# Turning the local attention result with whole-array matmuls, under a new hand-written order of steps

## The chip, the cores and the metric

The kernel runs on one core of a Trainium2 chip. The metric is the device time of that core in microseconds (us), the median of three runs. The profile is one execution taken by the hardware profiler. Its engines are PE (TensorE matmuls; PEld are its weight loads), DVE (VectorE), ACT (ScalarE), POOL (GpSimd) and SP (the queue that issues nearly all DMAs).

## The reference, cut to what matters

```python
# 8 batches, 8 heads, 576 positions, head size 64, factor 4
q_d, k_d, v_d = means over groups of 4 positions            # 144 positions
out_up   = repeat(softmax(q_d k_d^T / 8) v_d, 4)            # coarse attention
out_local = softmax(q k^T / 8 where |i - j| < 4) v          # band attention
x = out_up + out_local                                      # as (8, 576, 512)
theta = x @ w_theta
y = w_tok_r @ (x * cos(theta)) + w_tok_i @ (x * sin(theta)) # over positions
u = x + y
out = u + relu(u @ w_ch)
```

## The kernel before, in words

All eight batches run through the same chain of steps, and several batches are under way at once. What sets the order is a table written out by hand, `ORDER`: some 1190 words, each one step. The first two letters are the kind of step, the rest says where it goes: for steps on PE the PSUM bank or the two banks that it writes, for copies and casts the engine (v DVE, a ACT, g POOL), for loads the staging slot. The k-th word of a kind is the k-th batch and piece of that kind. `pin()` ties each engine's instructions to that order, so every engine, SP too, works strictly in the order of the words. A step whose input is late holds up all that stands behind it on its engine.

The steps of a batch, in the words used below:

- Loads on SP into 16 staging slots: `lk`, `lq` (k and q, 288 KB, L287), `lv` and `lw` (the two halves of a piece of v, 128 KB each, L347). A slot is loaded anew once its earlier content is cast.
- Casts to bf16: `ck`, `cq` (L295), `cv` (L396). `tp` turns k or q on PE (nine 128x128 transposes, L302), `ev` copies it out of PSUM (L315). `kd`, `qd` are the sums of four positions (two POOL instructions, L329 and L332 or L335, or one on DVE, L321).
- Coarse attention: `pv`, `vd` (means of v: PE L404 and L407, copy L412 and L415), `sd`, `ed` (scores L426, exponential on ACT L437), `nd`, `xn` (L447, L452; division on DVE), `xd`, `xc`.
- Local attention: `ps`, `ex` (scores L482, exponential L490), `mk` (band mask, on DVE L505 or on POOL L503 and L505), `po` (times v, L515), `nm` (division on DVE, L523 and L524, into `tmp`).
- `xt` (L537) turns the local result so that channels are on partitions, into PSUM. `xa` (L545, DVE) adds the coarse result on the way to `xT`.
- The rest: `th`, `cs` (theta on PE L556, cosine and sine on ACT), `xm`, `zz` (product with x), `mx`, `ua` (mixing over positions, 64 groups of nine 128x288 matmuls, L636, and the sum on DVE L641), `up`, `du`, `ch`, `rl` (the last matmul L666 and its relu on DVE L674), `st` (stores), `ht`, `rt` (the same for the last 64 positions of two batches).
- `wm` are matmuls of zeros that fill PE while it has nothing to do (L764).

Matmuls of `ps`, `sd`, `po` and `xt` use 64x64 quarters of the array, four at a time; nearly all others use the whole array.

Of the kernel before, what the change touches and what calls it, by code (L numbers as in the profile page):

```python
# [57 lines left out]
kcg l10 l11 l12 l13 kcv lk4 lq5 c1a wm7e0 kcg c1g t101 lk6 lk7 ckg c1a ckg c1v t123 e1a kcv e1v wm737 tp01 x12 cqa x13
lq8 x14 cka x15 cqg evv cva lk9 tp67 ckg cvv cva lqa lqb tp01 lk1 cqg x14 cva wm521 evv evv cqa qdv tp23 cva la3 eva
pv47 vda wm624 ps01 kdg la6 ps23 ex kdv ckg lq4 ex wm656 wm717 lq2 ps01 qdg lk5 sd67 mkv ckv cqg sd45 po23 ed lk8 cag  # L60
ed ex po67 lq9 lba nm cba nd45 nm nd23 xn cag mkg cqa tp01 po67 xn po45 nm lkb eva xd0 mkg ckg lq7 cka xca la1 po23 nm
tp67 cag xt45 la0 xt01 nm lb3 lb4 lb5 cqg lbc xa lba lb2 xt23 xa eva tp67 lb8 cqg lb1 caa ts th4 kdg cs cbg xm5 xa lv7
evv lw th0 th2 lv0 cbv lw zz cbg tt3 xm4 lv3 cs cbg cbv ct cbg cbg cs lvb lw lw wp0 wcv wp1 wcv ztg wp5 th3 wp1 lv8
wcv xm2 cbg xm0 zz zp7 tp45 cs qdg wp3 wp6 zz wcv lw zz wcv wcv zca eva wp7 wcv wp1 wca te wp0 wcv ps34 ps56 ex ex
ps12 mx0 lq1 cvg lk2 lka mx7 lqc mx3 qdv cvg ua lk7 ex ua lk0 mkv mkv kdg sd67 po45 nm sd12 lq4 cva lk5 lk9 cvg cvg ed
ed mx0 ua ua lq3 pv67 po45 po23 nm mx0 vda mkg nd67 lk8 nd45 lkb nm xn xn lq6 ckg ckg tp12 mx3 po45 ua lca ua nm cqg
cqg tp67 eva eva xd0 ckg ckg up1 lq7 po23 lvc xcv nm tp45 xt67 cqg mx0 cqg xt23 eva xt45 lv4 qdg kdg uca lw lv0 lw lw
lv3 lv1 lw lw xa xa tp67 cka ts ckg ckg th1 th2 xa th5 lk8 xm4 evv cs cqg xm1 ckv th3 zz tt4 up6 lq6 lqb cs zz tp12
xm7 ua cs ucv ct cs cqg eva te ztv xm6 zz zz mx0 ua tp34 zp7 tp56 ps12 zcv mx7 mx0 ex cvv kdg evv eva lk7 lk9 cvg lk4
qdg ua up7 uca sd12 mkv ps34 po56 ex ua ccv lcc lc5 kdg nm mkv mx0 sd34 ed po56 cvg cvg ua cqg mx7 nm ua ed mx0 ua lk2  # L70
cka cqg ps67 lqd lq0 cva po45 nm lca ex po23 ckg ckg nm pv01 lvb mx6 vda lk6 utv lw tp45 eva lv1 lw cca ccv nd01 nd23
ua xn xn qdg tp67 mx5 eva lv8 lv9 cqg cqg lw lw ccg ps34 qdg ps67 ua ps12 kdv ex ex xd0 lva xca lw mkg mkg lqc lq0 ch5
rl ckg ckg cvg cvg ch3 sd67 xt45 mkg ed rl ex ts mx0 xa xt67 po45 lv5 th1 cs xa nm ua tp23 th7 up4 up1 ucv xt56 xa mkv
lv4 ch0 eva po56 po23 cvg lq2 tt4 uca th1 cs th7 nm st nm xm2 lqb rl lq1 zz lqd ct cvg xm6 lw cqg ch5 cs zz cs cqa te
up0 up1 rl sd23 ucv po67 ch4 nm rl ch0 rl ucv tp67 lv7 ed cvg pv45 vdv lk8 lk9 eva st st tp23 eva xm0 ztg lk0 lka lw
xm1 zz zz zp7 ch6 zca lvc lv3 kdg nd45 xn nd23 ckg tp01 cva xn qdg utg mx7 cka ps23 rl kdg eva ps01 ua po45 mx6 up7 ex
ex lw lw lv8 nm qdg lw cqg po45 cqg ucv lvb lv2 lw sd23 sd01 lv5 ed mx7 lw lw ua tp23 nm xd4 ed ckg ckg xca st evv
tp01 eva mx6 mkg xt45 xt23 ua ua cva cvg cvg xt01 cka ts cvg xa xa mx7 th6 xa po45 nm pv23 tt0 th1 lk4 xm4 st st mkg
th5 vdv st cs nd23 ua zz ct cqg cqg ztg tp67 th4 cs dt po01 cs cs te xn evv po23 mx5 kdg qdg xm4 xm6 mx7 nm ps01 ex nm
ps23 ua lvd ua ex ch5 ps01 ex qdg zz lw lw xm7 zz rl kdg zp6 zz mkg nd23 xn lv1 lva lv3 mx5 zca sd67 lw ps01 ex po34  # L80
mx2 ua lw ed tp01 sd67 cva nm po34 eva cvv cvg ed lw up5 uca ua mx2 cvg nm cvg lvc xd3 ua pv04 xcv lk7 lk0 mx7 lq9 lq6
lq2 lqd lq8 lqb lq5 ckg ckg vda lq7 lw xt56 mkv cqg cqg po34 lk4 xt01 xa xa ch2 st cva ts lv6 th5 up6 ckg xm0 nm th1
# [5 lines left out]
evv mx1 ztg xd2 up0 ua cs ch3 rl cs te mx4 ch7 qdg ps56 rl xcv ua mx1 ex cvg po23 po45 ua uca ps67 ex ht1 nm nm st st
rt cva ss mx0 ua po67 xt45 nm ps23 st xa ex ts du kdg th1 xm0 xm7 cs th6 cs xm4 zz zz zz ch5 rl kdg mx7 ua th0 po67 nm
cs te xt45 xa sd12 ch3 xm0 ch7 ch4 xt56 st ed sd12 mkg mkg ed ts zz dz lw mx0 lv1 du du cvv lw cvg th1 cs rl uta mx3  # L90
st rl rl xa dxb ua po45 po67 pv02 nm nm ua du mx1 vda ch4 dx mkg ua po23 po01 po67 rl sr nm mx5 ua mx4 tt5 dx1 du nm
nm nd23 xn nd01 st mx6 th7 mx2 cs xn xd3 mx0 ua ua xcv ua ua xt67 utv ct dx st st xt45 xt23 xa ch1 rl th0 ch6 ch1 ch7
cs xa xa tt0 zz zz th2 th3 cs st du du ch4 rl zz zz ztg ct dz rl mx2 mx0 mx1 cs ua ua st dxe dx ht0 ua th1 cs th3 dx7
dx zz st st mx2 rl mx1 ua ua cs zz dt mx3 mx1 mx2 zz zz ztg dz mx7 ua mx3 du du du mx6 rt ua ua utg ua st rl du st mx7
mx4 ua ua ua sr mx7 mx6 mx5 ua ua ua du du ua ch7 ch6 ss ch5 rl rl ch7 ch6 ch4 ch3 du du st uta dt sta rl st rl ht7
ch2 sta rl st rl sta rl st rt ssa sr rl sta rm su k0
"""


# [1 line left out]
def kernel(  # L101
# [161 lines left out]
    at = {}  # L263
# [261 lines left out]
                                in0=ps[:, :, :, 0:D], in1=r.unsqueeze(3).to_broadcast([P, 2, 4, D]), op=ALU.mult)  # L525

    def xt(b, u, w):
        ps = at["xt", b, u] = pair(w).rearrange("p k (x n) -> p (k x) n", x=2)
        for i, c in enumerate(UNITS[u]):
            t = tmp[(NCH * b + c) % NTMP]  # L530
            for g in range(2):
                n = 2 * c + g
                lo = STEP * n - W0[n]
                for j in range(4):
                    for hf in range(2):
                        r = slice(W * hf, W * hf + W)
                        nc.tensor.matmul(out=ps[W * (j % 2):W * (j % 2) + W, 2 * hf + j // 2,  # L537
                                                CH * i + STEP * g:CH * i + STEP * g + OWN[n]],
                                         lhsT=t[r, g, D * j:D * j + D], rhs=ident[r, W * hf + lo:W * hf + lo + OWN[n]],
                                         start=True, stop=True)  # L540

    def xa(b, u, w):
        lo = 2 * CH * u
        cnt = min(2 * CH, S - lo)
        nc.vector.tensor_tensor(  # L545
            out=xT[b % 2][:, :, lo:lo + cnt].rearrange("p e (m j) -> p e m j", j=4),
            in0=at.pop(("xt", b, u))[:, :, 0:cnt].rearrange("p e (m j) -> p e m j", j=4),
            in1=xdT[b % 2][:, :, lo // 4:(lo + cnt) // 4].unsqueeze(3).to_broadcast([P, 4, cnt // 4, 4]),
            op=ALU.add)


# [256 lines left out]
```

## Time and profile before

| | |
|---|---|
| time, median of 3 runs | 230.54 us (230.37 to 230.74) |
| span of the profiled execution | 232.2 us (a time of its own for it is not shown) |
| PE busy | 217.7 us, 94% |
| DVE busy | 187.7 us, 81% |
| ACT busy | 156.2 us, 67% |
| POOL busy | 145.0 us, 62% |
| DMA queue q1 | 81.9% of 16 engines' span |

PE is busy for nearly the whole span, so what counts is how much work PE has and where it waits. In the first 30 us it waits for loads and for the first batch's chain; behind that its waits are short and scattered. Busy time includes the time in which the last matmul of a group drains, so a step of PE is better read from the chain of waits, which runs from end to end. Differences in span are taken over to the median one to one.

### The profile page before, as it was taken

Reading aid. Unit: us, or ns where it says so; the run is one execution under the profiler, and the core shown is the slowest. Engines: PE = TensorE matmul, PEld = TensorE weight load, DVE = VectorE, ACT = ScalarE, POOL = GpSimd, SP = SyncE. Lnnn points to the kernel's source line nnn. Section 1 sums busy time; section 2 is a strip of 40 time slices with the busy share of each in tenths; the row PEclk is TensorE's granted clock in tenths of the full one; section 3 lists DMA queues with packets and bytes.
Section 4 is the critical chain, followed back from the end, with each engine's and each line's share of the span. In section 5 each row is a group of like instructions: output and inputs, shape, how many; then the busy total and the mean of one; then the engine's idle time right before and its main releaser. Section 6 shows DMA issues by size and latency. Waiting matters only on the chain.

```text
span 232.2 us, 9404 instructions
## 1 busy us (share of the span) xinstructions
PE 217.7 (94%) x3943; PEld 152.6 (66%) x3970; DVE 187.7 (81%) x367; ACT 156.2 (67%) x243; POOL 145.0 (62%) x192
## 2 busy tenths in 40 slices
...
GB/s 217 395 390 390 291 114 238 361 300 118 265 391 179 165 245 285 243 142 214 205 165 347 307 213 115 206 153 92 67 149 109 71 127 193 138 159 137 142 227 245
DMA packets 76795, 49.41 MB, mean 213 GB/s; under 512 B 61136, under 2 KB 61392, under 8 KB 76752
## 3 DMA queue, kind: packets, MB, share of 16 engines
q1 hardware_dynamic: 76096, 47.76, 81.9%
q10 hardware_dynamic: 656, 1.05, 1.3%
q8 instruction: 31, 0.51, 0.9%
...
## 4 chain that ended last, share of the span: by engine, by line
PE 60%; DMA 10%; POOL 10%; issue 6%; ACT 5%; DVE 4%; SPq 4%; DVEq 0%; POOLq 0%; ACTq 0%
PE PS L636 21%; PE PS L666 9%; PE PS L556 8%; DMA st<-in_q_dram 6%; PE PS L302 4%; POOL two L329 3%; PE PS L515 2%; SPq L347 2%; DMA st<-in_k_dram 2%; PE PS L537 2%; DMA ur<-uT 2%; POOL q_tm L295 2%; PE PS L482 2%; PE PS L447 1%; PE PS L595 1%
## 5 line engine op out<-in xcount | busy, mean ns | idle before, releaser
L636 PE MATMUL PS<-WT,z 128*128 128x288 bf16 x576 | 78.0, 287 | 0.0
L636 PEld LDWEIGHTS <-z 128*128 128x128 bf16 x576 | 53.9, 98 | 15.9 <-issue 1.3
L641 DVE TENSOR_TENSOR uT<-PS,xT 128x288 bf16<-128x288 f32 x64 | 28.6, 452 | 12.7 <-PE PS L636 10.9
L561 ACT ACTIVATE cs<-PS,pihc 128x512 bf16<-128x512 f32 x32 | 22.0, 689 | 21.1 <-PE PS L556 13.4
L556 PE MATMUL PS<-wth,xT 128*128 128x512 bf16 x116 | 30.8, 383 | 0.7 <-issue 0.2
L666 PE MATMUL PS<-wch,uT 128*128 128x512 bf16 (+1 forms) x122 | 29.8, 373 | 0.9 <-issue 0.6
L524 DVE TENSOR_TENSOR tmp<-PS,rl 128x512 bf16<-128x512 f32 x40 | 27.7, 692 | 1.4
L545 DVE TENSOR_TENSOR xT<-PS,xdT 128x928 bf16<-128x928 f32 (+1 forms) x24 | 22.3, 952 | 3.7 <-PE PS L537 2.3
L674 DVE SCALAR_TENSOR_TENSOR osb<-PS,ur 128x512 f32<-128x512 f32 x28 | 19.1, 687 | 7.1 <-DMA ur<-uT 3.0
L490 ACT ACTIVATE pm<-PS 128x1024 bf16<-128x1024 f32 (+1 forms) x24 | 20.5, 880 | 6.2 <-PE PS L482 6.1
L577 POOL TENSOR_TENSOR zT<-xT,cst 128x512 bf16<-128x512 bf16 x7 | 9.7, 1383 | 20.6 <-ACT cst L574 20.6
L295 POOL CAST k_tm<-st 128x576 bf16<-128x576 f32 x23 | 15.1, 668 | 11.2 <-DMA st<-in_k_dram 11.1
L396 POOL CAST v_w<-st 128x512 bf16<-128x512 f32 x21 | 13.3, 651 | 10.6 <-DMA st<-in_v_dram 10.5
L770 ACT ACT_TABLE_LOAD x15 | 19.2, 1283 | 0.3
L666 PEld LDWEIGHTS <-uT 128*128 128x128 bf16 x132 | 11.9, 98 | 11.2
L562 ACT ACTIVATE cs<-PS 128x512 bf16<-128x512 f32 x32 | 19.1, 597 | 0.0
L556 PEld LDWEIGHTS <-xT 128*128 128x128 bf16 x128 | 11.7, 99 | 10.6 <-issue 0.6
L295 POOL CAST q_tm<-st 128x576 bf16<-128x576 f32 x23 | 15.4, 686 | 4.9 <-DMA st<-in_q_dram 4.7
L503 POOL TENSOR_TENSOR pm<-pm,band 128x512 bf16<-128x512 bf16 x16 | 18.3, 1164 | 0.0
L329 POOL TENSOR_TENSOR two<-qT 128x576 f32<-128x576 bf16 x14 | 16.5, 1177 | 0.7 <-ACT qT L315 0.4
L620 DVE TENSOR_TENSOR z<-PS,cs 128x1024 bf16<-128x1024 bf16 x24 | 15.8, 684 | 0.5 <-ACT cs L562 0.3
L437 ACT ACTIVATE pd<-PS 128x864 bf16<-128x864 f32 x16 | 13.8, 889 | 2.5 <-PE PS L426 2.5
...
## 6 DMA issues: line engine op xcount, KB each, us to landing
...
st<-in_v_dram SPq DMA_DIRECT2D x70, 128.0 KB, 5.2
...
```

Source lines behind the costliest of these rows:

```text
L295: COPY[w](out=to, in_=of)
L329: nc.gpsimd.tensor_tensor(out=t, in0=src[:, :, 0:2], in1=src[:, :, 2:4], op=ALU.add)
L490: nc.scalar.activation(out=pm[(3 * b + u) % NPM][:, :, 0:n].rearrange("p e c j w -> p e (c j w)"), in_=at.pop(("ps", b, u))[:, :, 0:4 * W ...
L524: nc.vector.tensor_tensor(out=tmp[(NCH * b + c) % NTMP].rearrange("p g (j d) -> p g j d", d=D), in0=ps[:, :, :, 0:D], in1=r.unsqueeze(3).t ...
L545: nc.vector.tensor_tensor(out=xT[b % 2][:, :, lo:lo + cnt].rearrange("p e (m j) -> p e m j", j=4), in0=at.pop(("xt", b, u))[:, :, 0:cnt].r ...
L556: nc.tensor.matmul(out=ps, lhsT=xT[b % 2][:, dc, P * c:P * c + P], rhs=wth[:, dc, :], start=(dc == 0), stop=(dc == 3))
L561: nc.scalar.activation(out=t[:, 0, :], in_=ps, func=AF.Sin, bias=pihc, scale=1.0)
L562: nc.scalar.activation(out=t[:, 1, :], in_=ps, func=AF.Sin, bias=0.0, scale=1.0)
L636: nc.tensor.matmul(out=ps, lhsT=z[b % 2][:, j, P * dc:P * dc + P], rhs=WT[:, j, cols], start=(j == 0), stop=(j == 8))
L641: nc.vector.tensor_tensor(out=uT[b % 2][:, dc, cols], in0=at.pop(("mx", b, i)), in1=xT[b % 2][:, dc, cols], op=ALU.add)
L666: nc.tensor.matmul(out=ps[:, cols], lhsT=uT[b % 2][:, dc, P * c:P * c + P], rhs=wch[:, dc, cols], start=(dc == 0), stop=(dc == 3))
L770: nc.scalar.activation(out=idle, in_=pihc, func=TABLE[kind])
```

## The change

`xt` no longer uses quarters of the array. A chunk's results of eight heads lie on all 128 partitions: two groups of heads on the two halves. Before, each head and each of two position groups had a matmul of its own, 16 for a chunk. Now one matmul takes all 128 partitions and two heads' 128 channels, against two shifted copies of the identity side by side (2 x 58 columns): 4 for a chunk, each writing into one bank. The two halves that were in two banks lie in one bank now, so `xa` reads PSUM in another order. `ORDER` is a new table: new order, staging slots, PSUM banks and engines for copies and casts.

```diff
-mx7 ua cvg cvv uca te po01 nm qdg kdg qdg sd56 ed po23 ua ch4 rl xd0 ch1 ztg lw nm up7 ch4 uca xca po23 dz xt67 rl evg
+dk8 ct lqd cs zz cvg ucv ua tp34 eva mkg qdg kdg ckg cqv kdv th5 xm7 qdg mx6 zz xcv ua uca cs rl mx1 po67 ua po45 sd23
...
     def xt(b, u, w):
-        ps = at["xt", b, u] = pair(w).rearrange("p k (x n) -> p (k x) n", x=2)
+        ps = at["xt", b, u] = pair(w).rearrange("p k (x n) -> p k x n", x=2)
         for i, c in enumerate(UNITS[u]):
             t = tmp[(NCH * b + c) % NTMP]
             for g in range(2):
                 n = 2 * c + g
                 lo = STEP * n - W0[n]
-                for j in range(4):
-                    for hf in range(2):
-                        r = slice(W * hf, W * hf + W)
-                        nc.tensor.matmul(out=ps[W * (j % 2):W * (j % 2) + W, 2 * hf + j // 2,
-                                                CH * i + STEP * g:CH * i + STEP * g + OWN[n]],
-                                         lhsT=t[r, g, D * j:D * j + D], rhs=ident[r, W * hf + lo:W * hf + lo + OWN[n]],
-                                         start=True, stop=True)
+                for k in range(2):
+                    nc.tensor.matmul(out=ps[:, k, :, CH * i + STEP * g:CH * i + STEP * g + OWN[n]],
+                                     lhsT=t[:, g, P * k:P * k + P], rhs=identw[:, :, lo:lo + OWN[n]],
+                                     start=True, stop=True)
 
     def xa(b, u, w):
...
-            out=xT[b % 2][:, :, lo:lo + cnt].rearrange("p e (m j) -> p e m j", j=4),
-            in0=at.pop(("xt", b, u))[:, :, 0:cnt].rearrange("p e (m j) -> p e m j", j=4),
-            in1=xdT[b % 2][:, :, lo // 4:(lo + cnt) // 4].unsqueeze(3).to_broadcast([P, 4, cnt // 4, 4]),
+            out=xT[b % 2][:, :, lo:lo + cnt].rearrange("p (x k) (m j) -> p x k m j", k=2, j=4),
+            in0=at.pop(("xt", b, u))[:, :, :, 0:cnt].rearrange("p k x (m j) -> p x k m j", j=4),
+            in1=xdT[b % 2][:, :, lo // 4:(lo + cnt) // 4].rearrange("p (x k) m -> p x k m", k=2).unsqueeze(4)
+            .to_broadcast([P, 2, 2, cnt // 4, 4]),
             op=ALU.add)
```

The words for each engine count as follows: casts of v on POOL 21 before and 28 now, on ACT 13 and 8, on DVE 6 and 4; masks on POOL 14 and 13; filler matmuls of 512 columns 27 and 19, beside a few shorter ones. All else keeps its number of instructions, and most of it its engine.

Three places in the new order.

First place, the head: ACT's queue around the first batch's exponentials, before and then now (qT0 and kT0 are copies of the turned q and k, vd0 the means of v, pm0 and pm1 the exponentials of the local scores).

```order
L315 COPY qT0_64<-PS_61 128x1152
L412 CAST vd0_72<-PS_61 128x8x64
L415 CAST vd0_72<-PS_61 32x4x64 x2
L490 ACTIVATE pm0_83<-PS_61 128x1024
L490 ACTIVATE pm1_84<-PS_61 128x1024
```

In the new order, at the same place on ACT:

```order
L315 COPY kT0_62<-PS_61 128x2x576
L315 COPY qT0_64<-PS_61 128x1152
L261 CAST uT0_111<-st_126 128x576
L490 ACTIVATE pm0_83<-PS_61 128x1024
L490 ACTIVATE pm1_84<-PS_61 128x1024
```

The copies of vd0 went to DVE, and a cast of a token weight took their place.

Second place, POOL's queue ahead of the coarse scores of batch 6 (q_tm1 is the cast of its last q, k_tm2 that of a k of batch 7, qd0 and kd0 its sums), before:

```order
L295 CAST k_tm2_76<-st_126 128x9x64
L295 CAST q_tm1_78<-st_126 128x9x64
L396 CAST v_w0_70<-st_126 128x8x64
L329 TENSOR_TENSOR two_80<-qT0_64 128x576
L335 TENSOR_TENSOR qd0_68<-two_80 128x288
L329 TENSOR_TENSOR two_80<-kT0_62 128x580
L332 TENSOR_TENSOR kd0_66<-two_80 128x2x5x29
```

In the new order, on POOL:

```order
L396 CAST v_w0_70<-st_126 128x8x64
L505 TENSOR_TENSOR pm1_84<-pm1_84,band_131 128x2x256
L329 TENSOR_TENSOR two_80<-qT0_64 128x576
L335 TENSOR_TENSOR qd0_68<-two_80 128x288
L329 TENSOR_TENSOR two_80<-kT0_62 128x580
L332 TENSOR_TENSOR kd0_66<-two_80 128x2x5x29
L295 CAST k_tm0_74<-st_126 128x9x64
```

The cast of batch 6's last q is now on ACT, away from the k of batch 7. The sums' last word, `qdg`, stood directly ahead of the scores `sd56` (the line of `ORDER` above); now two groups of `mx` and two `po` stand between it and `sd23`.

Third place, POOL's queue ahead of the means of v of batch 3 (pm2 is the mask of its second local unit, v_w1 the casts of its v, of which `pv` needs all five), before:

```order
L503 TENSOR_TENSOR pm2_85<-pm2_85,band_131 128x512 x2
L396 CAST v_w1_71<-st_126 128x8x64 x2
L295 CAST q_tm0_77<-st_126 128x9x64
L396 CAST v_w1_71<-st_126 128x8x64
L577 TENSOR_TENSOR zT_110<-xT0_101,cst_109 128x512
```

In the new order, on POOL:

```order
L503 TENSOR_TENSOR pm2_85<-pm2_85,band_131 128x512 x2
L396 CAST v_w1_71<-st_126 128x8x64 x2
L295 CAST k_tm0_74<-st_126 128x9x64
L295 CAST k_tm1_75<-st_126 128x9x64
L329 TENSOR_TENSOR two_80<-kT0_62 128x580
L332 TENSOR_TENSOR kd0_66<-two_80 128x2x5x29
L396 CAST v_w1_71<-st_126 128x8x64
```

Behind these, one k cast, the mask pm3, one v cast, two q casts and the fifth v cast follow on POOL before `pv` of batch 3 can start; before, the fifth v cast came three casts after the mask pm2.

More of the change, by code (lines that the diff above doesn't have):

```diff
@@ L57 @@
 ORDER = """
[L58 to L82, printed above, removed]
@@ L88 @@
[L88 to L96, printed above, removed]
+l10 l11 l12 l13 lk4 c1a lk5 ckg lk6 lq7 lq0 lk8 c1a c1a lq1 wm053 t101 e1v c1a ckg wm231 t123 cqg e1v cqg kcg wm431
@@ new lines @@
+tp01 x14 x15 lq2 x12 x13 cka evv cvv kdv cvv kcv x16 ckg cva cqg cva tp01 cqg lk9 la3 lb4 lb5 lb6 lk7 lq0 wm710 tp23
+kcg cva eva wm717 tp01 pv45 eva eva wm711 ps23 kcv kdv cba lb8 lq1 qdg la2 lba qdg lbb lq4 vdv ex mkv cbv ps01 wm751
+sd45 cbv po23 ex lkc ed ckg ckg lad po01 cbg cqg cqg la9 lb7 lk8 cbg cag lq0 nm mkv sd67 nm lb1 lba ps45 tp23 ed ex
+nd67 lv3 xn nd45 tp01 po67 xn cag mkg cbg cag nm eva ts eva wp2 po34 xd5 xca nm wcv cqa kdg qdg cbg wp6 lvb lvd lw lw
+xt01 cqg xa xt45 wca xa caa po23 wp7 lk0 wp6 th0 cbg th1 nm cbg cka wca xt23 xm7 th4 wcv ckv cs xa cs zz tp56 tt2 th7
@@ new lines @@
+xm3 cs ct tp01 xm2 wp4 cs evv lw ztg lva lv1 eva zz xm3 wp5 wp7 lw zz lw wp2 zp6 wca ps01 zz wcv te wp5 ex zcv wcv wcv
+ps34 wcv cvv kdg mx7 qdg mx2 ps01 mkv ckg cvg ex po56 ex cvg cvg cvg ua ua nm mx3 sd01 lk0 lqb ed po45 sd67 mx2 mkv
+po01 ed nm po45 ua pv36 mx7 nm nm ua ckg xt01 vda lkd lq3 nd34 cqa ts nd56 ua xn xn mx7 tp23 lk7 lq8 ua xd5 lqa lk1
+lvc xcv lk9 lw xa lqb lk0 lq4 lk2 mx7 lc6 lq5 lve eva cka cka lv7 mkg lw cqg xt45 cqg tp23 lw lv8 po01 th6 xa tp45 eva
+lqd lw lv3 th2 xm3 ua nm lw lkf cs xt67 qdg ckg evv cqa th0 cs cs tp45 lc1 xm2 eva lka xa zz xm3 tt6 th7 mx0 ps45 xm1
@@ new lines @@
+cvg kdg cqg ckv zz zz cqv ct cs ztv ckg ckg kdg up6 lv2 lq0 lcb lc4 lk9 qdg zp7 tp23 zz cvg zcv ucv ua ex eva mx1 ua
+tp67 eva te mkv tp45 evv mx1 sd23 ps67 po45 mx0 nm up4 ex cvv ed cva ua mx5 uca ua mkv sd12 po67 ps34 cqg kdg nm kdg
+ccg ckg cqg ua ckg ed ex cva utg mx0 po67 po45 nm ua pv23 nm vda mx1 up0 ua ucv tp67 nd45 tp01 eva xn nd23 mx6 ps45 xn
+ps23 lw lv8 lqf lkd lka lk3 cca qdg ccg cqg qdg eva lw lvb cca mkv ua xd0 up1 ex lw lq4 xcv ch7 lv0 lv1 lw lq6 uca rl
+xt45 xa xt01 mx6 ch7 cqg ckg ex xa sd45 ps01 ua ex po23 ed utv mkv th6 nm cs th0 xt12 rl tp34 xa mkg cvg cvg ch7 evv
```

26 lines of the change are left out of this document (22 added, 4 removed).

## Prediction

> **What bounds the kernel now.** I read the page first, then the busy time by stretches, the chain of waits, and the timeline where PE waits.
>
> ```profile
> PE 217.7 (94%) x3943; PEld 152.6 (66%) x3970; DVE 187.7 (81%) x367; ACT 156.2 (67%) x243; POOL 145.0 (62%) x192
> 20.00:25.00 5.00, 3.64 (x102) 3.15 (x101) 4.54 (x13) 3.83 (x6) 5.00 (x7) 0.99 1.05 337
> 25.00:30.00 5.00, 4.78 (x103) 3.45 (x104) 4.68 (x6) 4.31 (x7) 3.89 (x7) 0.67 0.98 276
> 40.00:80.00 40.00, 39.66 (x887) 29.96 (x888) 35.94 (x69) 33.74 (x51) 33.24 (x43) 1.00 0.95 257
> 80.00:120.00 40.00, 38.89 (x827) 27.92 (x831) 35.71 (x71) 33.81 (x51) 36.95 (x47) 1.00 1.00 217
> 120.00:160.00 40.00, 37.20 (x697) 26.21 (x703) 32.85 (x61) 31.87 (x54) 26.62 (x27) 1.00 0.99 216
> 160.00:200.00 40.00, 38.70 (x674) 24.88 (x679) 32.30 (x64) 21.74 (x38) 13.82 (x15) 1.00 0.52 116
> ```
>
> The columns behind the stretch are the busy times of PE, PEld, DVE, ACT and POOL, then the granted clock, the DMA share and GB/s. PE sets the pace from 40 us on: it idles 0.34 + 1.11 + 2.80 + 1.30 = 5.55 us of 160. DVE and ACT are next, at 80 to 90%. POOL has 37 of 40 us in the second stretch, so a longer queue on POOL would show there. The profiled span of 232.2 us stands 1.7 us over the median of 230.54; I sum differences and take them off the median.
>
> **The turning itself.** The change takes out 640 matmuls of quarters and puts in 160 of the whole array with 116 columns.
>
> ```profile
> L537 PE MATMUL PS<-ident,tmp 64*64 64x58 bf16 (+1 forms) x640 | 8.7, 198 | 0.0
> 99.47 0.50 PE PS L302 x9
> 100.23 0.51 PE PS L302 x9
> 100.74 1.10 PE PS L636 x9
> 101.84 0.79 PE PS L537 x80
> 102.63 1.21 PE PS L636 x9
> ```
>
> In the chain a batch's 80 quarter matmuls take 0.79 us. The group of `mx` behind them takes 1.21 us and the one ahead 1.10: going from quarters to the whole array costs about 0.1 us, and going in about as much, which lies within the 0.79. So a batch is 0.69 us of matmuls, and eight are 5.5 us. Nine transposes of 128 columns take 0.50 us, 56 ns each; 116 columns are 116/128 of that, 51 ns, and 160 of them 8.1 us. That is +2.6 us. Against it stand the changes of form. I counted in both orders where PE goes from one size of tile to another: 107 before, 81 now, since `xt` no longer breaks up whole-array work and the other quarter steps stand in closer groups. 26 times 0.1 us is -2.6 us. The two cancel: I take 0, within -0.5 and +0.5, which also covers two runs of 58 columns against one run of 128.
>
> The Trainium skill says in "TensorE: Matmul & The Clock Gate" (Back-to-back issue gap) that a stream of weight loads and matmuls of 128 columns sustains about 81 ns each. By that, 160 matmuls of 116 columns take 73 ns each, 11.7 us instead of 8.1, and the sum below would end at +2.8 us instead of -0.8. The rows above have such a stream at 56 ns, so I go by the trace; the case itself is a rival below.
>
> `xa` moves the same 928 elements, from two banks in turn. Its row:
>
> ```profile
> L545 DVE TENSOR_TENSOR xT<-PS,xdT 128x928 bf16<-128x928 f32 x16 | 17.7, 1120 | 3.7 <-PE PS L537 2.3 <-PE PS L482 1.3
> L315 DVE COPY kT<-PS 128x1152 bf16<-128x1152 bf16 x3 | 4.1, 1351 | 0.8 <-PE PS L302 0.8
> ```
>
> A DVE copy that reads PSUM in strides takes 1.17 ns per element, `xa` 1.21: order has hardly a price here, and I take 0. Up to 5% more would be 24 x 0.05 = 1.2 us of DVE, in a queue with 10% to spare. The fillers lose eight matmuls of 512 columns, some 1.8 us of PE; they stand where PE waits for loads (DMA share 1.05 at 20 us), so this too is 0. Their cover is the clock, a rival below.
>
> **The head.** The first batch's loads come in the same amounts and as early, so the scores of batch 0 start as before.
>
> ```profile
> 14.20 1.12 ACT L315 COPY qT<-PS 128x1152 bf16<-128x1152 bf16 x1 [0.36 <-PE PS L302]
> 15.22 0.59 ACT L412 CAST vd<-PS 128x512 bf16<-128x512 f32 x1
> 15.69 0.74 ACT L415 CAST vd<-PS 32x256 bf16<-32x256 f32 x2
> 16.45 1.94 ACT L490 ACTIVATE pm<-PS 128x1024 bf16<-128x1024 f32 x2
> 20.30 0.69 ACT L261 CAST uT<-st 128x576 bf16<-128x576 f32 x1
> ```
>
> The copies of `vd` hold ACT from 15.22 to 16.45 us. Now a token weight's cast of 0.69 us stands there, and the exponential starts about 16.0 instead of 16.45. Masks, division and turning follow it, so I take -0.5 us; 0 if the loads decide further on, -1.3 (0.59 + 0.74) if the cast fits elsewhere.
>
> **Waits that the new order loosens.** Three places hold most of the 2.80 us lost between 120 and 160.
>
> ```profile
> 134.20 0.66 POOL L295 CAST k_tm<-st 128x576 bf16<-128x576 f32 x1 [3.83 <-DMA st<-in_k_dram]
> 134.81 0.67 POOL L295 CAST q_tm<-st 128x576 bf16<-128x576 f32 x1
> 135.53 0.68 PE L302 MATMUL PS<-ident,q_tm 128*128 128x128 bf16 x9 [0.81 <-POOL q_tm L295]
> 141.88 0.26 PE L426 MATMUL PS<-qd,kd 64*64 64x144 bf16 x4 [0.27 <-POOL qd L335]
> 153.88 0.32 PE L515 MATMUL PS<-v_w,pm 64*64 64x65 bf16 x16 [0.83 <-DVE pm L505]
> ```
>
> POOL stands 3.83 us for a k of batch 7, and the last q of batch 6 is queued behind it: PE waits 0.81. The scores of batch 6 wait 0.27 for POOL's sums, and its first `po` 0.83 for the mask on DVE. In the new order that q is cast on ACT, 5 us of PE work ahead of its transposes; 2.6 us of PE work stand between the last sum and the scores; the mask is on POOL, 6 us ahead of `po`. Together -1.9 us. What is late next at these places I can't see; 0 if it comes as late.
>
> For the rest of the 5.55 us, 3.6, I counted from batch 1 on the steps of PE whose producer stands with less PE work ahead of it than the producer takes (masks, casts, sums, products for `mx`, means of v): 36 before, 25 now. 11/36 of 3.6 is -1.1 us, with 0 and -2.2 as ends, since most such places cost nothing in the trace.
>
> **Waits that it brings.** The third place of the new order: POOL from the mask of batch 3 to its fifth v cast.
>
> ```profile
> L503 POOL TENSOR_TENSOR pm<-pm,band 128x512 bf16<-128x512 bf16 x16 | 18.3, 1164 | 0.0
> L295 POOL CAST q_tm<-st 128x576 bf16<-128x576 f32 x23 | 15.4, 686 | 4.9 <-DMA st<-in_q_dram 4.7
> L295 POOL CAST k_tm<-st 128x576 bf16<-128x576 f32 x23 | 15.1, 668 | 11.2 <-DMA st<-in_k_dram 11.1
> L329 POOL TENSOR_TENSOR two<-kT 128x580 f32<-128x580 bf16 x13 | 15.0, 1152 | 0.4
> L396 POOL CAST v_w<-st 128x512 bf16<-128x512 f32 x21 | 13.3, 651 | 10.6 <-DMA st<-in_v_dram 10.5
> L577 POOL TENSOR_TENSOR zT<-xT,cst 128x512 bf16<-128x512 bf16 x7 | 9.7, 1383 | 20.6 <-ACT cst L574 20.6
> L332 POOL TENSOR_TENSOR kd<-two 128x290 bf16<-128x290 f32 x13 | 8.7, 671 | 1.0
> L505 POOL TENSOR_TENSOR pm<-pm,band 128x512 bf16<-128x512 bf16 x6 | 6.9, 1152 | 0.0
> st<-in_v_dram SPq DMA_DIRECT2D x70, 128.0 KB, 5.2
> 79.67 0.86 PE PS L556 x4
> 85.33 0.86 PE PS L666 x4
> ```
>
> 2 x 1.16 + 5 x 0.65 + 3 x 0.67 + 2 x 0.69 + 1.15 + 0.67 + 1.15 is 11.9 us, and it starts behind an exponential of 1.0 us. PE has 11.4 us of work in the order between that exponential and `pv` of batch 3: eight blocks of `th` and `ch` at 0.86, two of transposes at 0.50, and 3.5 us of smaller steps. So `pv` waits 12.9 - 11.4 = 1.5 us, and with it all of PE. In batch 5 the same comes again: from its first v cast POOL has 11.3 us (one mask of two parts, one of one, three v, one product of 1.38, one sum, two k and two q) until the fourth v cast ends, and PE has 9.5 until `pv`: 1.8 us, of which I count half, 0.9, since PE's first wait has let POOL catch up. Nothing of this is in the trace of before; the ends are 0 (POOL starts earlier than PE's place in the order says) and 4.3 (both in full, and 1.0 in batch 6, where a v load of 5.2 us stands on SP behind the transposing DMA of `dz`, which waits for POOL).
>
> **The end.** The last steps swap places.
>
> ```profile
> 227.08 0.69 DVE L704 SCALAR_TENSOR_TENSOR st<-PS,utr 128x512 f32<-128x512 f32 x1 [0.17 <-PE PS L700]
> 227.95 0.76 DVE L674 SCALAR_TENSOR_TENSOR st<-PS,ur 128x256 f32<-128x256 f32 x2 [0.18 <-PE PS L666]
> ```
>
> Before, half a chunk of relu (0.76/2) was the last work on DVE; now it is `rt`, 0.69: +0.3 us.
>
> **The sum.** 0 (turning) - 0.5 (head) - 1.9 - 1.1 (loosened) + 1.5 + 0.9 (POOL) + 0.3 (end) = -0.8 us: 230.54 - 0.8 = 229.7 us.
>
> **The rivals.**
>
> Larger gain, 227.3: POOL runs ahead and neither `pv` waits, so the 2.4 us fall away. For it: POOL idled 3 us of 40 at 80 to 120, but 13 and 26 in the stretches behind. Against: its casts wait on loads, 11.1 and 10.5 us in the rows above.
>
> No change, 230.5: behind each of the three loosened waits the next producer is as late, -1.9 becomes -1.0 or so, and the 0.8 is gone. For it: DVE and ACT are 80 to 90% full at the same places.
>
> Slower, 232.6: POOL's queues set the pace of `pv` in batches 3, 5 and 6, 4.3 us instead of 2.4 (+1.9), and the -1.1 of uncounted places doesn't come (+1.1), so 229.7 + 3.0. The sign turns when PE's waits at `pv` sum to 3.2 us. For it: 28 casts of v on POOL for 21, 7 x 0.65 = 4.6 us more, where the row of 80 to 120 has POOL at 36.95 of 40. Against: from 40 to 80 POOL has only 33.24.
>
> Clock, 231.4: the row of 25 to 30 us has a clock of 0.67, which is 3.3 us at half speed and costs 1.7; it follows a stretch in which PE was busy 3.64 of 5 us. With fewer fillers a second one could come. Against: up to the first `mx` the new order has as much real work on PE. The Trainium skill says in "TensorE: Matmul & The Clock Gate" (Why this matters for your kernels) that idle gaps over about 3 us bring the half clock; no gap of the row before it can be that long (1.36 us idle in all), so here shorter waits did.
>
> Whole-array matmuls dearer, 233.4: the weight load, and not the columns, sets their pace.
>
> ```profile
> L302 PEld LDWEIGHTS <-q_tm 128*128 128x128 bf16 x126 | 7.5, 98 | 2.7 <-POOL q_tm L295 1.5 <-issue 0.6
> ```
>
> A load takes 98 ns; half way between 51 and 98, at 74, 160 matmuls cost 3.7 us more. Against: the transposes have the same loads and run at 56. The 81 ns of the Trainium skill ("TensorE: Matmul & The Clock Gate", Back-to-back issue gap) would be this case.
>
> **How the numbers follow.** Forecast 0.36 (228.6 to 230.3), larger gain 0.15, no change 0.18, slower 0.21, clock 0.06, dearer matmuls 0.04. 0.2% (0.46 us) is about what a measurement of this kernel can tell from no change. Faster is the larger gain and most of the forecast (0.34): 0.49. Same is no change and the forecast's upper edge: 0.19. Slower is the rest: 0.32. The range reaches to 226.9, half a us below the larger gain, and to 232.8, just over the slower rival.
>
> **What the profile after would show.** `xt` of a batch as 20 matmuls in about 1.0 us in the chain, `mx` behind it at 1.10. The exponential of batch 0 at 16.0 us on ACT. No wait of L302 on a q cast, of L426 on sums or of L515 on a DVE mask between 120 and 160. Waits of L404 (`pv`) on POOL's v casts in batches 3 and 5, or none, which would be the larger gain. I am wrong in the sum if PE idles over 7 us between 40 and 200 (slower) or under 4 (larger gain), and wrong in the turning if its matmuls stand over 60 ns apart.

## The result, and the profile after

After takes 237.45 us (median of four, 236.29 to 238.57) against 230.64 for before in the same job: a ratio of 1.029, interval 1.024 to 1.034. In three later jobs it stood at 1.034, 1.037 and 1.042. The forecast was 229.7, with a range up to 232.8: wrong in sign and by some 8 us. Medians are of all executions of a job; the ratios leave out those that are over 1.5% above the fastest of their kernel. The profiled execution of after took 237.72 us, with a span of 236.0: the time is 1.7 us over the span. Every run gives both numbers, and the difference is 1.7 to 1.8 in each, but for one execution (2.5, the profiled one of e6).

The rows of after that answer to those shown of before, from the busy time by engine on the page and by stretches:

```profile
PE 217.5 (92%) x3457; PEld 154.5 (65%) x3483; DVE 185.4 (79%) x361; ACT 157.2 (67%) x239; POOL 148.4 (63%) x200
```

```profile
25.00:30.00 5.00, 4.87 (x67) 3.24 (x65) 4.93 (x10) 5.00 (x10) 4.84 (x7) 1.00 1.09 328
40.00:80.00 40.00, 38.64 (x753) 29.82 (x756) 36.13 (x67) 31.80 (x48) 33.42 (x44) 1.00 1.05 260
80.00:120.00 40.00, 39.41 (x719) 28.66 (x722) 32.91 (x65) 35.46 (x55) 34.54 (x44) 1.00 0.97 232
120.00:160.00 40.00, 37.57 (x617) 27.45 (x621) 31.91 (x61) 30.25 (x48) 28.60 (x33) 1.00 0.85 190
160.00:200.00 40.00, 39.47 (x555) 26.42 (x560) 32.17 (x64) 22.26 (x36) 16.68 (x19) 1.00 0.52 118
```

PE is as busy as before, 217.5 us, and from 40 to 200 us it idles 4.91 us where the profile of before had 5.55. By these two profiles the middle hasn't changed, and the spans differ by 3.8 us where the medians differ by 6.8. So these rows alone do not tell the loss. PE's waits in after tell more (what it waited for, us in total, times, the longest). The list has those that bear on the loss; left out are the 1.3 us at the start (L226), which every run has, and several of 0.7 us or less in the first 60 us:

```profile
PE PS L634 <- DVE osb L672: 2.3, 1, 2.3
PE PS L482 <- issue: 1.1, 1, 1.1
PE PS L664 <- DVE st L672: 0.8, 1, 0.8
PE PS L554 <- ACT ur L651: 0.8, 1, 0.8
PE PS L426 <- POOL qd L335: 0.7, 1, 0.7
PE PS L515 <- issue: 0.5, 1, 0.5
PE PS L535 <- issue: 0.3, 1, 0.3
```

(In after `xt` is L535, `mx` L634, `th` L554, `ch` L664, the sum behind `mx` L639, the product `zz` of the last two batches L613, the transposing DMA of x, `dx`, L603.) Two things in it were in no term and no rival of the forecast. The longest wait stands at the end of the program; its place in the timeline:

```profile
198.81 1.22 SPq L603 DMA_TRANSPOSE st<-xT  x1
200.71 5.04 SPq L603 DMA_TRANSPOSE st<-xT  x3
204.70 2.37 PE L634 MATMUL PS<-WT,z 128*128 128x288 bf16 x18
207.09 0.69 DVE L613 TENSOR_TENSOR z<-st,cs 128x1024 bf16<-128x1024 bf16 x1 [6.93 <-DMA st<-xT]
207.70 0.45 DVE L639 TENSOR_TENSOR uT<-PS,xT 128x288 bf16<-128x288 f32 x1
208.67 1.28 DVE L672 SCALAR_TENSOR_TENSOR osb<-PS,ur 128x512 f32<-128x512 f32 x2
209.41 1.26 PE L634 MATMUL PS<-WT,z 128*128 128x288 bf16 x9 [2.33 <-DVE osb L672]
```

The first product of batch 7 stands in DVE's queue ahead of the second to fifth evacuation (`ua`) of batch 6 and of three relus. It needs the four transposing DMAs, the last of which is through at 207. DVE stands for 6.93 us, PE's banks fill up, and PE stops.

The other is the waits on "issue", where PE waited for nothing that the profile shows. They lie inside a group of equal matmuls, where no semaphore is waited for. The same three places in after, in after run again (e5) and in a third program with the same PE instructions up to there (e3), from the timelines of PE:

```profile
79.61 0.23 PE L515 MATMUL PS<-v_w,pm 64*64 64x65 bf16 x5 [0.53 <-issue]
101.14 0.47 PE L535 MATMUL PS<-ident,tmp 128*128 128x116 bf16 x6 [0.32 <-issue]
121.86 0.23 PE L482 MATMUL PS<-qT,kT 64*64 64x64 bf16 x5 [1.14 <-issue]
```

```profile
80.15 0.23 PE L515 MATMUL PS<-v_w,pm 64*64 64x65 bf16 x5 [0.30 <-issue]
102.34 0.48 PE L535 MATMUL PS<-ident,tmp 128*128 128x116 bf16 x6 [0.99 <-issue]
122.86 0.23 PE L482 MATMUL PS<-qT,kT 64*64 64x64 bf16 x5 [0.95 <-issue]
```

```profile
104.75 0.48 PE L535 MATMUL PS<-ident,tmp 128*128 128x116 bf16 x6 [3.60 <-issue]
```

Each time five, six and five matmuls of the group are left: the stop belongs to an instruction. In the trace the first of these instructions are numbers 2749, 3514 and 4280 of PE, 765 and 766 apart; in a later record that lacks none, 2755, 3523 and 4291, 768 apart, three times 256. The page lists an instruction queue of 27 packets and 0.44 MB, 16 KB each. Taking these packets' times from the trace, PE goes on 1.4 to 1.6 us behind the landing of one (here 1.58, 1.50 and 1.41 us). So PE's program comes in pieces of 256 instructions. The packet of a piece starts when PE is about to enter the piece ahead of it, or later (0.9 us before at the earliest, in e13 to e15, whose records lack no matmul). Between 55 and 125 us it landed 3.3 us after PE had entered, in the mean, and 5.3 at most, in after's profile. If PE passes the 256 instructions ahead in less than landing plus 1.4, it stops. I call this a code stop.

### The profile page after: what moved, and what is told of

The parts are those of the page before. It is cut to its first block, busy times and chain, and to the rows that moved or that the text cites. A ratio compares the mean times of both kernels' runs of the same rounds, so it can differ in the third digit from the quotient of the medians.

```text
span 236.0 us, 8416 instructions
## 1 busy us (share of the span) xinstructions
PE 217.5 (92%) x3457; PEld 154.5 (65%) x3483; DVE 185.4 (79%) x361; ACT 157.2 (67%) x239; POOL 148.4 (63%) x200
## 4 chain that ended last, share of the span: by engine, by line
PE 71%; DVE 8%; DMA 5%; issue 4%; ACT 4%; SPq 3%; POOL 2%; DVEq 0%; POOLq 0%; ACTq 0%
PE PS L634 26%; PE PS L664 10%; PE PS L554 10%; PE PS L302 4%; PE PS L515 3%; PE PS L535 3%; DMA st<-in_k_dram 2%; PE PS L482 2%; PE PS L593 2%; PE PS L447 2%; DMA ur<-uT 2%; SPq L603 2%; PE PS L452 1%; DVE pm L505 1%; PE PS L648 1%
## 5 line engine op out<-in xcount | busy, mean ns | idle before, releaser
L634 PE MATMUL PS<-WT,z 128*128 128x288 bf16 x576 | 78.9, 286 | 2.5 <-DVE osb L672 2.3
L634 PEld LDWEIGHTS <-z 128*128 128x128 bf16 x576 | 54.1, 98 | 19.2 <-issue 4.4
L639 DVE TENSOR_TENSOR uT<-PS,xT 128x288 bf16<-128x288 f32 x64 | 28.3, 450 | 11.8 <-PE PS L634 11.4
L554 PE MATMUL PS<-wth,xT 128*128 128x512 bf16 x118 | 30.8, 379 | 1.4 <-ACT ur L651 0.8
L664 PE MATMUL PS<-wch,uT 128*128 128x512 bf16 (+1 forms) x121 | 29.8, 372 | 1.6 <-DVE st L672 0.8
L329 POOL TENSOR_TENSOR two<-qT 128x576 f32<-128x576 bf16 x15 | 18.1, 1209 | 11.7 <-ACT qT L315 5.8
L542 DVE TENSOR_TENSOR xT<-PS,xdT 128x928 bf16<-128x928 f32 (+1 forms) x24 | 22.5, 950 | 2.9 <-issue 1.4
L575 POOL TENSOR_TENSOR zT<-xT,cst 128x512 bf16<-128x512 bf16 x7 | 8.1, 1160 | 23.4 <-ACT cst L572 23.4
L396 POOL CAST v_w<-st 128x512 bf16<-128x512 f32 x28 | 18.0, 656 | 4.9 <-DMA st<-in_v_dram 4.3
L664 PEld LDWEIGHTS <-uT 128*128 128x128 bf16 x132 | 12.2, 98 | 11.8 <-issue 1.1
L554 PEld LDWEIGHTS <-xT 128*128 128x128 bf16 x128 | 11.5, 98 | 11.4 <-issue 1.2
L618 DVE TENSOR_TENSOR z<-PS,cs 128x1024 bf16<-128x1024 bf16 x24 | 16.3, 683 | 2.8 <-PE PS L593 2.6
L503 POOL TENSOR_TENSOR pm<-pm,band 128x512 bf16<-128x512 bf16 x14 | 15.9, 1160 | 2.2 <-ACT pm L490 2.2
L654 POOL COPY ut<-uT 128x256 bf16<-128x256 bf16 x7 | 2.8, 401 | 21.2 <-DVE uT L639 21.2
```

The source lines that it names most:

```text
L329: nc.gpsimd.tensor_tensor(out=t, in0=src[:, :, 0:2], in1=src[:, :, 2:4], op=ALU.add)
L542: nc.vector.tensor_tensor(out=xT[b % 2][:, :, lo:lo + cnt].rearrange("p (x k) (m j) -> p x k m j", k=2, j=4), in0=at.pop(("xt", b, u))[:, ...
L554: nc.tensor.matmul(out=ps, lhsT=xT[b % 2][:, dc, P * c:P * c + P], rhs=wth[:, dc, :], start=(dc == 0), stop=(dc == 3))
L634: nc.tensor.matmul(out=ps, lhsT=z[b % 2][:, j, P * dc:P * dc + P], rhs=WT[:, j, cols], start=(j == 0), stop=(j == 8))
L639: nc.vector.tensor_tensor(out=uT[b % 2][:, dc, cols], in0=at.pop(("mx", b, i)), in1=xT[b % 2][:, dc, cols], op=ALU.add)
L664: nc.tensor.matmul(out=ps[:, cols], lhsT=uT[b % 2][:, dc, P * c:P * c + P], rhs=wch[:, dc, cols], start=(dc == 0), stop=(dc == 3))
```

## The experiments

Theory A: the loss sits in the place of the products at the end. Theory D: code stops. Rivals: the turning itself, or late data. A time is given against before in the same job, with the ratio's interval; a difference in us behind a ratio is worked out from it.

**e1, the turning alone.** Before's order, with the new `xt` and `xa` (as in the diff above).

> The order of before, with only the turning and the sum behind it written anew (whole-array matmuls of 116 columns). Theory A (the loss is in the new order, and a step of the turning costs what the trace shows): 160 matmuls at 51 to 52 ns for 5.5 us of quarters are +2.6 us, and in this order only 5 changes of tile size go (107 to 102) at 93 ns, -0.5: +2.1 us, 232.7. Rival B (the turning itself is what made after slow, by some effect on DVE or the clock that the matmul steps don't show): +5 us or more, 235.5 and up. Rival C (PE's waits swallow it): +0 to +0.7.

231.88 us, ratio 1.0073 (1.0042 to 1.0104), +1.7 us. Theory A held: the turning is 2.8 us of matmuls less 5 changes of tile size, and is not what made after slow.

**e2, the old turning in the new order.**

> The new order, with the old turning in quarters. Theory A: the quarters are 2.6 us less of matmuls, but 38 more changes of tile size (119 for 81) at 93 ns are +3.5: +0.9 us over after, 238.4. Rival B (the turning made after slow): about before's time, 231 to 233. Rival C (waits decide): 237.5.

240.91 us, ratio 1.047 (1.040 to 1.053), above after's 1.029 to 1.042. The rival is out: with the old turning the new order is no faster. That it is slower, as the count of changes says, is likely by the medians; the interval is too wide for its size. In e1 and e2 the pieces of code begin elsewhere too (code stops of 0.8 and 4.9 us in their profiles), so neither time is the turning's alone.

**e3, the products later.**

```diff
-dx1 mx1 dx zz ua ztg zz rl rl zz dz dt zz ua rl du ua du ua mx2
+dx1 mx1 dx ua ztg rl rl dz dt ua rl du ua du ua zz zz zz zz mx2
```

> After, with one thing moved: DVE's four products of batch 7 (zz) stand behind the fifth evacuation (ua) of batch 6 instead of ahead of the second. Theory A (DVE stands 6.9 us for the last transposing DMA of x of batch 7, and the evacuations and the relus queued behind it stop PE for 2.5 us): the DMA lands at 207.1, PE has 4.2 us of work left to the first mx of batch 7, the four products take 2.7: the stop goes, -2.3 to -2.5 us, 235.0. Rival B (the end is bound by the DMA queue on SP behind it, the transposes du of batches 6 and 7 and the stores): -0.5 or less.

239.67 us (235.86 to 255.42), ratio 1.029 (1.019 to 1.040): by the time alone no gain is shown. The timeline shows the stop gone; it is the place shown of after:

```profile
204.84 4.45 SPq L603 DMA_TRANSPOSE st<-xT  x3
208.66 3.47 PE L634 MATMUL PS<-WT,z 128*128 128x288 bf16 x27
211.07 0.46 DVE L639 TENSOR_TENSOR uT<-PS,xT 128x288 bf16<-128x288 f32 x1 [0.57 <-PE PS L634]
211.44 2.49 DVE L613 TENSOR_TENSOR z<-st,cs 128x1024 bf16<-128x1024 bf16 x4
212.83 1.39 PE L634 MATMUL PS<-WT,z 128*128 128x288 bf16 x10
```

But the code stop of 3.60 us shown above stood at 104 us of the same execution, and behind it 3.4 us at half clock. That can hide a gain of this size in the time of four executions, and it led to the shifts below.

**e4, before again.**

> Before, unchanged, for spans and clock of its executions beside its times, and a second profile. Theory A (the profile of before held a half-clock stretch of 1.65 us at 25 to 30 us that its timed runs lack): time 230.6, span 1.7 under the time as in after, about 229, and no half-clock stretch in the profile. Rival B (the stretch is there in every execution): span 232, time 230.6 to 234.

230.56 us, ratio 1.001 (0.997 to 1.005). Its profiled execution took 229.12, span 227.4, without a half-clock stretch:

```profile
40.00:80.00 40.00, 39.77 (x884) 30.10 (x875) 35.95 (x70) 33.91 (x50) 35.41 (x46) 1.00 0.94 268
80.00:120.00 40.00, 39.63 (x845) 28.74 (x847) 35.95 (x71) 34.54 (x52) 35.54 (x45) 1.00 0.93 239
120.00:160.00 40.00, 39.42 (x795) 27.93 (x797) 34.73 (x68) 34.25 (x57) 29.57 (x30) 1.00 0.85 177
160.00:200.00 40.00, 38.92 (x588) 25.07 (x593) 30.29 (x59) 18.90 (x34) 10.71 (x11) 1.00 0.54 124
```

Here PE idles 2.26 us from 40 to 200, not 5.55, and 0.58 from 120 to 160, not 2.80. The first profile of before showed an execution of about 233.9 us (its span of 232.2 and the 1.7), 3.4 over the median. Theory A held: no half-clock stretch. But the stretch (3.4 us at half speed, so 1.7 us) is only a part of what sets the two profiles 4.8 us apart; PE's waits from 40 to 200 us are 3.3. Against this profile the middle of after is worse by 2.6 us.

**e5 to e8, where the pieces begin.** e5 is after unchanged. e6 and e7 put 70 fillers of 64 columns in the head for a group of six, 128 PE instructions more; e7 has e3's edit too. e8 adds 16 such fillers to before, 32 instructions.

```diff
-lbb lq4 vdv ex mkv cbv ps01 wm751 sd45
+lbb lq4 vdv ex mkv cbv ps01 wm701 wm701 wm701 wm701 wm701
...
+wm701 wm701 sd45
```

> After, unchanged, on the same chip as the runs beside it, for its spread and a second profile. PE's code comes in pieces of 16 KB; in the profile of after PE stood 0.72, 0.53 and 1.33 us in the middle of groups, at PE instructions 2749, 3514 and 4280 of the record, 765 and 766 apart, each time until 1.4 to 1.6 us behind the landing of such a piece. Theory D (code loading): stops of PE stand at some of the same places, 2749 and 255 or its multiples further, 1.5 to 6 us in all, and differ from run to run; the other waits are the same to 0.5 us. Rival E (late data): they stand at other places, behind a named producer. Time 236 to 239.

> After, with one filler group in the head (six matmuls, ahead of the coarse scores of batch 0) put in by 70 fillers of 64 columns, 27 ns each: 128 PE instructions more, so each piece of 16 KB begins half a piece earlier in the work. Costs 0.8 us of PE at 17 us, where PE waits 0.7 for sums anyhow: 0 to +0.8. Theory D: the three stops at the old places go, and the new pieces are passed more slowly (by after's own times only 1.1 us are missing to 5.2 us per piece, for 4.5 us before): stops of 0 to 1 us in all, time -1.5 to -3 against after, 234 to 236. Rival E (the stops are waits for data): the same stops at the same work, time +0 to +1.

> Both edits: the products zz of batch 7 behind the fifth evacuation of batch 6, and the 70 small fillers. Theory D with A (the end's stop of 2.5 us goes, the code's stops go): -4 to -5.5 against after, 232 to 233.5, steadier than the run with the products alone (235.9 to 255). Rival E: the gain of the end alone, if it shows at all, -0 to -2.5.

> Before, with 16 fillers of 64 columns more in the head (32 PE instructions, 0.45 us of PE at 17 us). Theory D: before is fast by where its pieces begin. With 32 more instructions four pieces are passed in 3.2 to 3.7 us and ten in under 5.2 by its own times, so 11.4 us are missing to 5.2 for 4.9 now: PE stops where a piece of code begins, 2 to 6 us in all, time +2 to +5, 232.5 to 235.5. Rival E: +0 to +0.5.

e5: 239.47 us, ratio 1.034 (1.026 to 1.043), with stops at the three places and one at 26 us. e6: 238.74, ratio 1.031 (1.021 to 1.041). e7: 237.75, ratio 1.029 (1.022 to 1.037); its one profile is of an execution of 434 us with PE at under half its pace throughout, and is not used. e8: 236.51, ratio 1.024 (1.016 to 1.033), +5.6 us for 0.45 us of work (+6.0 by the medians). In e6 and then e8 (lines of e6 stand four lower than in after, those of e8 one lower than in before):

```profile
23.82 0.25 PE L456 MATMUL PS<-vd,pd 128*72 128x130 bf16 x1 [1.82 <-issue]
100.91 0.32 PE L470 MATMUL PS<-ident,xdn 72*128 72x72 bf16 x5 [1.60 <-issue]
121.73 0.26 PE L519 MATMUL PS<-v_w,pm 64*64 64x65 bf16 x8 [0.85 <-issue]
```

```profile
23.65 0.25 PE L516 MATMUL PS<-v_w,pm 64*64 64x65 bf16 x6 [1.06 <-issue]
55.05 0.40 PE L303 MATMUL PS<-ident,q_tm 128*128 128x128 bf16 x4 [1.01 <-issue]
80.67 0.25 PE L538 MATMUL PS<-ident,tmp 64*64 64x58 bf16 x7 [0.84 <-issue]
```

In e6 the stops left `xt` and the scores, and stand in other work at the same instruction numbers (705, 3515, 4281). Theory D is shown, and late data is out. But my size for e6 was wrong, its time is not clear of e5's: I counted only how fast PE passes a piece, and the landings differ as much. e8 is the plainest: 16 fillers that cost next to nothing by their work make before nearly as slow as after, and its profile, with 5.4 us of code stops, has no half-clock stretch before the last 0.3 us.

**e9, before with the products early.** The mirror of e3. In this program the evacuation of one group of batch 6 (the third) reads its bank after `th1` was written there, so that batch's output differs; nor does `th1` wait for that evacuation any more.

```diff
-ht0 ua th1 cs th3 dx7 dx zz st st mx2 rl mx1 ua ua cs zz dt mx3 mx1 mx2 zz zz
+ht0 th1 cs th3 dx7 dx cs zz zz zz zz ua st st mx2 mx1 rl ua ua dt mx3 mx1 mx2
```

> Before, with the order of DVE at the end as after has it: the four products zz of batch 7 stand ahead of the third to fifth evacuation of batch 6 (and of one relu), instead of between and behind them. PE's program is unchanged. Theory A (a product that waits for the transposing DMA of x holds the evacuations behind it, and PE with them): in the first profile of before that DMA lands at 205.5, the four products take 2.7 to 208.3, the evacuation that frees the bank of the sixth group ends at 208.8, and PE is there at 206.7: +2.1, and up to +3 if the next group waits as well; 232.6 to 233.5. Rival (PE has other work there, or the queue of DMAs on SP bounds the end anyhow): +0 to +0.7.

231.55 us, ratio 1.0043 (1.0012 to 1.0075), +1.0 us. The wait is there, with 1.46 of the 2.1 expected:

```profile
201.78 2.51 DVE L615 TENSOR_TENSOR z<-st,cs 128x1024 bf16<-128x1024 bf16 x4 [2.76 <-DMA st<-xT]
204.72 8.51 PE L636 MATMUL PS<-WT,z 128*128 128x288 bf16 x68 [1.46 <-DVE uT L641]
```

**e10, before with 16 fillers fewer** (`wm737`, `wm521`, `wm624` and `wm656` taken out).

> Before, without 16 of its 33 filler matmuls (those at 10 to 17 us; the 14 of the start stay): 32 PE instructions fewer, PE's pieces of code begin 32 instructions later in the work, 2.9 us less of PE in a stretch where it waits for loads. Theory D (where the pieces begin decides): by before's own times 5 pieces are passed in under 5.2 us for 9 now, 3.7 us are missing for 4.9: time -0.3 to -1, 229.6 to 230.2. Rival (the fillers cover the clock): a stretch at half clock in the head, +0.5 to +2. Rival (PE's stops depend on the loads alone): 0.

232.37 us, ratio 1.0107 (1.0072 to 1.0142), +2.5, where theory D had forecast a gain. In its profile code stops sum to 4.0 us, and the clock was granted in full (1.00 in each row from 10 to 30 us). But of the nine executions in the ratio seven have a mean clock of 0.994 or less (one stretch of 3.4 us at half clock makes 0.993), and of before's 63 in the later jobs only three. So the rival, that the fillers cover the clock, is not out: 16 fillers fewer cost time, and this run does not tell the pieces from the clock.

**e11 and e12, the end in order, beside after.** e3's edit, and the last steps as in before.

```diff
-ch3 rl rm sta rl ht0 st su rt sta sr ssa k0
+ht0 ch3 rl sta st rt ssa sr rl sta rm su k0
```

> After, with its end in order: the products zz of batch 7 behind the fifth evacuation of batch 6, and the last steps as in before (the last group of four tails ahead of the last chunk in two halves). Theory A: by PE instruction the products' place was worth 4.0 to 4.25 us between instruction 6600 and the end (the two profiles of the same program up to there), and the last steps 0.5: -4 to -4.7 against after in the same job. Rival (code loading eats it): -1 or less.

> After, unchanged, for the comparison with the run beside it on the same chip: 236 to 240 as so far; stops at PE instructions 704, 2749, 3514, 4280 again (theory D), and the same 3 to 4 us lost from instruction 6600 to the end (theory A).

e11 237.87 us, ratio 1.030 (1.024 to 1.036); e12 238.96, ratio 1.037 (1.032 to 1.042). The swap of the last steps was a mistake of mine: the last tails now wait 1.4 us for a relu that frees their bank, and eat a good part of the gain.

**e13 to e15, the edit alone, after, and the edit with 96 PE instructions more** (54 fillers of 64 columns for the same six).

> After, with the products zz of batch 7 behind the fifth evacuation of batch 6 and nothing else. Theory A: -3.5 to -4.3 us against after in the same job. Rival (what is gained there is lost behind it, at the last transposing DMAs): -1 or less.

> After, unchanged, beside the other two: 236.5 to 240, with stops where PE's pieces of code begin of 2.5 to 6 us.

> The edit of the products, and one filler group of the head (six matmuls) put in by 54 of 64 columns: 96 PE instructions more. Theory D: from the landings and passing times of the pieces in the runs so far, about 2.2 us are lost at their beginnings for 3.6 now, and 0.3 to 0.8 us more of PE in the head: -0.6 to -1.4 against the edit alone. Rival (the place of the pieces matters little here): 0 to +0.5.

e13 237.42 us, ratio 1.031 (1.025 to 1.036); e14 239.13, ratio 1.042 (1.037 to 1.048); e15 235.12, ratio 1.023 (1.019 to 1.027). By the medians of the executions that the ratios take (236.81, 239.13 and 235.12) the edit gained 2.3 us, less than I expected, and the shift another 1.7, a little more than expected; both together 4.0. The shift did more than move the pieces: all five of e13's executions in the ratio have a mean clock of 0.994 or less, and none of e15's six. Time lost to the clock, estimated as (1 - clock) times the time, is 2.0 us in e13's mean and 0.5 in e15's, so the 1.7 can't be put down to the pieces alone.

Programs with the same PE instructions up to the end can be compared instruction by instruction. How much later the edited program reached a weight load of PE (number of 3483), in us:

```
                      3300     3450     last
e3  less e5          +2.92    -1.33    -1.06
e11 less e12         -3.18    -7.24    -5.49
e13 less e14         +1.75    -2.57    -1.66
```

From 3300 to 3450 the products' place is worth 4.25, 4.06 and 4.32 us. Not all of that is PE's stop. The edited programs take 20.0 us for this stretch, e5, e12 and e14 24.0 to 24.3, and after's first profile 22.5. In the three the granted clock is 0.50 for 3.41 us, from 210.2, 215.0 and 211.3 us on, in PE's stop of 2.2 to 2.8 us or up to 1.3 us behind it; in the first, with a stop of 2.3, it is 1.00 until 234.9. The rows of after, of e14 at that stretch and of e12 behind its stop at 105 us (the granted clock is the third number from the end):

```profile
205.00:234.00 29.00, 23.11 (x159) 15.40 (x158) 17.64 (x34) 2.16 (x4) 0.80 (x2) 1.00 0.73 177
211.40:214.60 3.20, 3.20 (x13) 1.66 (x12) 3.04 (x7) 0.00 (x0) 0.00 (x0) 0.50 0.08 16
105.80:109.10 3.30, 3.18 (x20) 2.33 (x19) 1.48 (x3) 1.69 (x2) 2.02 (x4) 0.50 0.04 9
```

So the place costs 2.5 us, and some 1.7 more where half clock follows. A part of the gain is lost again: from load 3300 to the last load it is 3.98, 2.31 (with the swap) and 3.41, and to the end of the span 3.4, 1.9 and 2.3. What differs ahead of 3300 is chance: code stops differ, e3 and e12 have a half-clock stretch behind their stops of 3.6 us at 105 us, e11 and e13 one between 22 and 30 us. (e12's profile is of an execution of 242.9 us, 4 over its median.)

Code stops in each profile (at a beginning, ending 1.2 to 1.75 us behind a landing; from start to start of PE's instructions, so each some 0.2 over the idle time in the rows), in us:

```
before's PE program:  before 1.6   e4 0     e9 1.7
shifted by +32, -32:  e8 5.4       e10 4.0
after's PE program:   after 2.6    e5 4.0   e12 4.6   e14 3.0   e3 3.8   e11 2.8   e13 3.8
shifted by 128, 96:   e6 5.5       e15 1.8
before, new turning:  e1 0.8       after, old turning: e2 4.9
```

No version beat before.

## Why the prediction was wrong

Two steps failed. The 3.0 us of gain came from waits of one profiled execution that before's later profiles (e4, e9) do not have, and what the new order costs, DVE's products in front of evacuations and the loading of PE's code, stood in no term of the sum. By its own steps:

- **Turning, 0: right, to 0.3.** The matmuls of `xt` stand in the chain as said, 52 ns apart, and an `mx` right behind them takes 1.10:

```profile
75.75 0.84 PE PS L535 x16
76.58 1.10 PE PS L634 x9
```

  In steps of PE it is 5.3 to 8.1 us of matmuls, +2.8, against 27 changes fewer (I had counted 26). Where a group in another form follows a matmul of `mx`, the step is 94 ns longer by the median (216 for 122), so -2.5. The 81 ns of the Trainium skill ("TensorE: Matmul & The Clock Gate", Back-to-back issue gap) do not hold for these matmuls. `xa` takes 1.12 us for 1.12: its price of 0 was right.

```profile
L542 DVE TENSOR_TENSOR xT<-PS,xdT 128x928 bf16<-128x928 f32 x16 | 17.5, 1116 | 2.1 <-issue 1.4 <-PE PS L535 0.5
```

- **Head, -0.5: wrong.** The cast took the place of the `vd` copies, but the copy of q ahead of it starts at 14.98 us for 14.20, and the exponential at 16.59 for 16.45, later and not earlier:

```profile
14.98 1.12 ACT L315 COPY qT<-PS 128x1152 bf16<-128x1152 bf16 x1
16.00 0.68 ACT L261 CAST uT<-st 128x576 bf16<-128x576 f32 x1
16.59 1.94 ACT L490 ACTIVATE pm<-PS 128x1024 bf16<-128x1024 f32 x2
```

- **Loosened waits, -1.9 and -1.1: wrong, since they weren't there to be gained.** The waits on the q cast, the sums and the mask are of the one execution profiled. In e4's list of waits none of the three is left at its place. It begins with these (the fourth row, four times 0.2 us on "issue", is left out), of which the first stands in every run:

```profile
PE PS L226 <- DVE warm L197: 1.3, 1, 1.3
PE PS L302 <- POOL k_tm L295: 0.9, 1, 0.9
PE PS L466 <- ACT kT L315: 0.7, 1, 0.7
PE PS L447 <- ACT pd L437: 0.5, 1, 0.5
PE PS L515 <- ACT pd L437: 0.3, 1, 0.3
```

  The step that failed is "I sum differences and take them off the median": the profile stood 3.4 us over the median, and I took 3 us of gain from waits that were a part of those 3.4. The prediction said that the span was 1.7 over the median, and did not ask why.

- **POOL at `pv`, +2.4: didn't come.** After's list has no wait of L404 on POOL. Here the larger-gain rival was right, but there was nothing for it to add to. (The slower rival's 229.7 + 3.0 is 232.7, not 232.6, and the chances of same and slower are each 0.01 off their parts; neither bears on the outcome.)
- **The end, +0.3: the swap was right, the end was missed.** From PE's last weight load to the end of the span it is 5.3 us in after's first profile and 4.8 to 4.9 in the other three, and 4.7 in e4. But 2.5 to 4.3 us stand ahead of it, at the products. I had counted steps of PE whose producer is late, and took masks, casts, sums, products and means. A DVE instruction that waits for a DMA, with PE's evacuations queued behind it, was not in that count.
- **Code loading: in no term and no rival.** The row of the instruction queue was on the page. In the profiles it is 2.6 to 4.6 us in after for 0 to 1.7 in before, some 2.4 us in the means. The Trainium skill says in "Runtime: NRT & Kernel Launch" (Instruction fetch mechanics) that code comes in blocks of 256 instructions, and that crossing one is "mostly hidden". The 256 agree with the 768 between stops; hidden it is not here, with stops up to 3.9 us.
- **Clock, a rival at 0.06: it came, though mostly not in the head.** After's first profile has no half-clock stretch before 234.9 us. But e5, e12 and e14 have one at the products, e12 another behind its code stop, and e11 and e13 one in the head. Of after's 19 executions in the ratios 16 have a mean clock of 0.994 or less, of before's 63 three; (1 - clock) times the time is 1.9 and 0.5 us in the means. So by this estimate some 1.4 us of the loss are half clock, and in the profiles of after each stretch stands at a stop of PE of over 2 us. Whether the eight fillers fewer have a part in it no run shows; e10 speaks for it.

What stands now for the 6.8 to 8.7 us, as the profiles give it: 2.5 at the products, 2.4 in code stops, some 1.4 of half clock, 0.2 behind PE's last weight load, and about 1 in smaller waits that after has and e4 has not, as the 0.8 for ACT's copy of `ur`: some 7.5 us. That the products' place and the beginnings of pieces cost time is shown by edits (e13 gained 2.3 us, e8 lost 5.6); their shares in after are read from the profiles. And e15 still stands 4.7 us over before, of which only 1.8 are code stops in its profile; the rest of that is open.
